# Folding softmax row sums on GpSimd instead of TensorE in a grouped-query attention block

## The chip, the cores and the metric

The kernel runs on one core of one Trainium2 chip. The metric is the device time of one execution in microseconds (us). Engines are called as in the profile: PE is TensorE, DVE is VectorE, ACT is ScalarE, POOL is GpSimd, SP is SyncE, which here issues almost all loads. PEld is TensorE's weight load, and a q behind an engine's name (SPq) marks its queue of instructions. Within 2% counts as the same.

## The reference

Two independent attention blocks, A and B, each on its own inputs, with the results side by side:

```python
q = (x @ wq)                      # x: 16 x 32 x 1024, wq: 1024 x 4096 -> 32 heads of 128
scores = q @ k^T * 128 ** -0.5    # 4 key/value heads, 512 cached keys, 8 query heads share each
p = softmax(scores)
out = (p @ v) @ wo                # wo: 4096 x 1024
```

All inputs are bfloat16. One *slot* of the kernel is one pair of batch and key/value head: 512 keys against 8 x 32 = 256 query columns. There are 64 slots for A and 64 for B.

## The kernel before

Scores are computed transposed, with keys on partitions, so the softmax sums run over partitions. There is no maximum: the exponent gets a constant shift, and a check at the end guards it. In each slot PE does four score matmuls and four value matmuls, and between them a stream of projection matmuls (`units`) is fed in, six or seven to a slot. The sums are formed in three steps: DVE reduces each 32 x 32 block of the exponentials (`partial_sums`), then the four key chunks of a pair of slots (`chunk_sums`), and PE adds the four partition quadrants with a matmul against stacked identities (`fold_sums`). That matmul also spreads the result to all quadrants. Of the tiles named below, kT holds the transposed keys and v_sb the values of a group of four slots, p_sb the exponentials of one slot; blk is the pool of the weights and of what the projections read and write.

```python
def load_k(j): ...   # one group j = 4 slots; kT tile from a pool of 3, DMA transposes on nc.sync
def load_v(j):
    v_sb = v_tiles[j] = kv.tile([P, GRP, KC, DH], BF16, name="v_sb")     # pool of 3
    nc.sync.dma_start(out=v_sb[:], in_=...)
# ... cut ...
def chunk_sums(j): ...            # DVE: parts -> cs
def fold_sums(j):
    sums = pair[j] = psum.tile([P, 2 * REP], FP32, name="sums", tag="sums", bufs=1)
    nc.tensor.matmul(sums[:], lhsT=fold[...], rhs=cs[...], start=True, stop=True)
def reciprocals(j): ...           # DVE: rall = 1 / sums, then transpose to r
def values(i): ...                # PE: 4 matmuls into ob, ONE PSUM bank for a pair of slots
def normalize(j): ...             # DVE: oT = r * ob, frees ob
# ... cut ...
for j in range(2, 2 * NG // GRP):
    at(GRP * (j - 1), load_k, j)          # at(slot, ...): place in program order
    at(GRP * (j - 1) + 2, load_v, j)
for c4 in range(3, 16): ...               # wq tiles of 1 MB, blk pool
for nh in range(NH):
    for hg in range(HKV):                 # wo tiles of 1 MB, blk pool
        at(NG - 12 + nh * 8 + hg * 2, load_wo, 0, nh, hg)
        at(NG + 20 + nh * 18 + hg, load_wo, 1, nh, hg)
# ... cut ...
for i in range(total_slots + 3):
    j, odd = divmod(i, 2)
    if live: do_loads(i); scores(i)
    run(units, 1)
    if not odd and 1 <= j <= NG: chunk_sums(j - 1)
    if i >= 3: values(i - 3)
    if odd and 1 <= j <= NG: reciprocals(j - 1)
    if not odd and j >= 2: normalize(j - 2)
    run(units, 5)
    if not odd and 1 <= j <= NG: fold_sums(j - 1)
    if live: partial_sums(i)
    run(units, 1 - (i % 4 == 3))
```

A load's place in this plan orders it in the SP queue. It is issued when SP has got that far and the buffer that it overwrites has been read for the last time.

## Time and profile before

Time before: 350.65 us, the median of three runs (350.25 to 350.69).

The page's first part gives the span and the busy time of each engine, with its share of the span and its number of instructions.

```profile
span 349.1 us, 5460 instructions
...
PE 340.7 (98%) x2163; PEld 221.0 (63%) x2204; DVE 283.4 (81%) x421; ACT 179.6 (51%) x196; POOL 8.9 (3%) x21
```

PE is busy all the time. Its lines in the timeline show start, length, engine, source line and operands; matmuls overlap, so the starts are what to subtract.

```profile
101.71 0.60 PE L371 MATMUL s_ps<-qT,kT 128*128 128x256 bf16 x4
...
102.80 1.24 PE L312 MATMUL q_ps<-xT,wq_sb 128*128 128x512 bf16 x5
103.69 0.36 PE L407 MATMUL sums<-cs,fold 128*128 128x16 f32 x1
103.91 0.39 PE L312 MATMUL q_ps<-xT,wq_sb 128*128 128x512 bf16 x1
104.14 0.60 PE L371 MATMUL s_ps<-qT,kT 128*128 128x256 bf16 x4
...
106.31 0.60 PE L371 MATMUL s_ps<-qT,kT 128*128 128x256 bf16 x4
```

A slot goes from one group of score matmuls (s_ps) to the next. (A few matmul records are missing from this trace, among them one projection matmul after 102.1; its weight load is listed at 102.04. So the first slot has seven.) The slot at 101.71 holds a fold (103.69) and lasts 2.43 us; the one at 104.14 has one projection matmul fewer and no fold and lasts 2.17 us. Over 28 periods of four slots (34.73 to 298.45 us) the mean is 9.42 us.

The groups of instructions give busy time and the mean of one in ns, then the idle time before them and what ended it.

```profile
L407 PE MATMUL sums<-cs,fold 128*128 128x16 f32 x64 | 22.9, 357 | 0.1
L399 DVE TENSOR_REDUCE cs<-parts 128x16 fp32r<-128x64 f32 x64 | 16.9, 264 | 2.2
L416 DVE RECIPROCAL rall<-sums 128x16 f32<-128x16 f32 x64 | 14.1, 220 | 0.0
L407 PEld LDWEIGHTS sums<-cs,fold 128*128 128x128 f32 x64 | 12.1, 190 | 8.3 <-DVE cs L399 0.9
```

The fold is 22.9 us of listed matmul time. Because matmuls overlap, that is not its price. The last number of the last line: twice PE's weight load waited for the chunk sums, 0.9 us in all.

### The profile page before, as it was taken

How to read it: one execution, taken by the hardware profiler on the slowest of the kernel's cores; microseconds unless marked ns; L12 is line 12 of the kernel's file. 1: busy time of each engine (PE TensorE's matmuls, PEld its weight loads, DVE VectorE, ACT ScalarE, POOL GpSimd, SP SyncE). 2: the span in 40 equal slices, each digit the busy share in tenths (PEclk: the TensorE clock that was granted, in tenths of full speed). 3: DMA queues.
4: the chain of work that ended last, by engine and by line, in shares of the span. 5: the costliest groups of instructions: out<-in, count | busy, mean ns of one | idle time of the engine just before them, and what ended most of it. 6: DMA issues, size and time to landing. Idle time of an engine off the chain costs nothing.

```text
span 349.1 us, 5460 instructions
## 1 busy us (share of the span) xinstructions
PE 340.7 (98%) x2163; PEld 221.0 (63%) x2204; DVE 283.4 (81%) x421; ACT 179.6 (51%) x196; POOL 8.9 (3%) x21
## 2 busy tenths in 40 slices
PE   8999999999999999999999999999999999999995
PEld 4556666666666666666666666666666666666554
DVE  2218888988988898898889999999989999899710
ACT  2247667666666666666654454454454445445000
POOL 0000000000000000000000000000000000000010
PEclk9999999999999999999999999999999999999999
DMA  7999999999996999999999659996579975400000
GB/s 242 275 251 339 181 274 264 254 269 249 270 214 176 199 233 233 296 275 210 305 313 192 175 126 289 348 199 122 135 258 287 284 182 97 116 17 0 15 32 20
DMA packets 125085, 71.70 MB, mean 205 GB/s; under 512 B 73632, under 2 KB 124064, under 8 KB 125056
## 3 DMA queue, kind: packets, MB, share of 16 engines
q1 hardware_dynamic: 122848, 68.24, 81.1%
q0 software_dynamic: 720, 1.97, 1.6%
q10 hardware_dynamic: 1488, 1.11, 1.1%
q8 instruction: 18, 0.29, 0.4%
q14 instruction: 11, 0.09, 0.1%
HBM read 51.38 MB, written 2.10 MB: 153 GB/s over the span
## 4 chain that ended last, share of the span: by engine, by line
PE 94%; DMA 3%; issue 1%; DVE 1%; ACT 0%; SPq 0%
PE f_ps L331 31%; PE q_ps L312 30%; PE ob L431 16%; PE s_ps L371 16%; DMA wq_sb<-in_A_wq_dram 2%; DMA x_sb<-in_A_x_dram 1%; DVE parts L390 0%; PE sums L407 0%; DVE o_sb L343 0%; ACT o_sb L341 0%; DVE cs L399 0%; PE ok_ps L614 0%; SPq L651 0%
## 5 line engine op out<-in xcount | busy, mean ns | idle before, releaser
L379 ACT ACTIVATE p_sb<-s_ps,shift 128x1024 bf16<-128x1024 f32 x128 | 142.5, 1114 | 113.1 <-PE s_ps L371 100.4
L390 DVE TRANSPOSE_TENSOR_REDUCE parts<-p_sb 128x32 f32<-128x1024 bf16 x128 | 158.2, 1236 | 21.5 <-ACT p_sb L379 20.9
L331 PE MATMUL f_ps<-wo_sb,oT 128*128 128x512 bf16 (+1 forms) x524 | 127.9, 367 | 0.4
L312 PE MATMUL q_ps<-xT,wq_sb 128*128 128x512 bf16 x475 | 124.8, 380 | 0.6
L371 PE MATMUL s_ps<-qT,kT 128*128 128x256 bf16 x512 | 76.8, 273 | 0.9
L431 PE MATMUL ob<-p_sb,v_sb 128*128 128x256 bf16 x512 | 76.8, 273 | 0.6
L331 PEld LDWEIGHTS <-oT 128*128 128x128 bf16 x544 | 53.0, 98 | 33.8
L312 PEld LDWEIGHTS <-wq_sb 128*128 128x128 bf16 x496 | 48.3, 98 | 35.1 <-DMA wq_sb<-in_A_wq_dram 0.6
L371 PEld LDWEIGHTS <-kT 128*128 128x128 bf16 x512 | 56.9, 113 | 20.9
L431 PEld LDWEIGHTS <-v_sb 128*128 128x128 bf16 x512 | 50.1, 98 | 19.8 <-DVE oT L453 0.3
L453 DVE TENSOR_TENSOR oT<-r,ob 128x512 bf16<-128x512 f32 x64 | 43.9, 685 | 12.7 <-PE ob L431 9.3
L320 ACT CAST qT<-q_ps 128x512 bf16<-128x512 f32 x62 | 36.1, 583 | 23.7 <-PE q_ps L312 20.8
L418 DVE STREAM_TRANSPOSE r<-rall 128x512 f32<-128x512 f32 x64 | 45.5, 711 | 2.2
L407 PE MATMUL sums<-cs,fold 128*128 128x16 f32 x64 | 22.9, 357 | 0.1
L343 DVE CAST o_sb<-f_ps 128x512 bf16<-128x512 f32 (+1 forms) x16 | 10.8, 673 | 10.8 <-PE f_ps L331 10.0
L399 DVE TENSOR_REDUCE cs<-parts 128x16 fp32r<-128x64 f32 x64 | 16.9, 264 | 2.2
L407 PEld LDWEIGHTS sums<-cs,fold 128*128 128x128 f32 x64 | 12.1, 190 | 8.3 <-DVE cs L399 0.9
L345 POOL DMA_DIRECT2D out_dram<-o_sb x15 | 8.2, 549 | 329.7 <-DVE o_sb L343 299.0
L416 DVE RECIPROCAL rall<-sums 128x16 f32<-128x16 f32 x64 | 14.1, 220 | 0.0
L341 ACT CAST o_sb<-f_ps 128x256 bf16<-128x256 f32 x1 | 0.4, 372 | 22.1 <-PE f_ps L331 22.1
L497 DVE COPY xT<-xT_ps 128x512 bf16<-128x512 bf16 x4 | 1.7, 424 | 5.3 <-PE xT_ps L493 5.3
L484 PE MATMUL warm_ps<-warm 128*128 128x512 bf16 x10 | 4.2, 580 | 1.3 <-DVE warm L230 1.3
(26 smaller groups left out, 22.8 us busy)
## 6 DMA issues: line engine op xcount, KB each, us to landing
v_sb<-in_A_v_cache_dram SPq DMA_DIRECT2D x16, 512.0 KB, 4.9
wq_sb<-in_B_wq_dram SPq DMA_DIRECT2D x8, 1024.0 KB, 6.5
wo_sb<-in_A_wo_dram SPq DMA_DIRECT2D x8, 1024.0 KB, 7.6
v_sb<-in_B_v_cache_dram SPq DMA_DIRECT2D x16, 512.0 KB, 4.2
wo_sb<-in_B_wo_dram SPq DMA_DIRECT2D x8, 1024.0 KB, 9.2
wq_sb<-in_A_wq_dram SPq DMA_DIRECT2D x7, 1024.0 KB, 8.0
out_dram<-o_sb POOLq DMA_DIRECT2D x15, 128.0 KB, 3.1
kT<-in_A_k_cache_dram SPq DMA_TRANSPOSE x64, 4.5
```

What stands on the lines that cost most here:

```text
L312: nc.tensor.matmul(ps[:], lhsT=w[:, dc, (h % 4) * DH:(h % 4 + 1) * DH], rhs=xT[pr][:, dc, :], start=(dc == 0), stop=(dc == DC - 1),)
L320: nc.scalar.copy(out=qT[pr, g][:, :, hl, :], in_=ps[:].rearrange("p (b s) -> p b s", s=SQ),)
L331: nc.tensor.matmul(ps[:, 0:width], lhsT=oT[pr, tt][:, h, :], rhs=wo_tiles[pr, nh, h // REP][:, h % REP, off:off + width], start=(h == 0), ...
L371: nc.tensor.matmul(s_ps[:, c, :], lhsT=kT[:, i % GRP, c, :], rhs=qT[pr, g][:, b, :, :].rearrange("p h s -> p (h s)"), start=True, stop=True,)
L379: nc.scalar.activation(out=p_sb[:], in_=s_ps[:], func=ACTF.Exp, bias=shift[:], scale=SCALE)
L390: nc.vector.tensor_reduce(out=parts[j][:, q, :, :].rearrange("p c h -> p (c h)"), in_=st[i]["p"][:].rearrange("p c (h s) -> p (c h) s", s=SQ),
L399: nc.vector.tensor_reduce(out=cs[:], in_=parts.pop(j)[:].rearrange("p q c h -> p q h c"), axis=AX.X, op=ALU.add,)
L407: nc.tensor.matmul(sums[:], lhsT=fold[:].rearrange("p r s -> p (r s)"), rhs=cs[:].rearrange("p q h -> p (q h)"), start=True, stop=True,)
L416: nc.vector.reciprocal(out=rall[:, j, :], in_=pair.pop(j)[:])
L418: nc.vector.transpose(out=r[:].rearrange("p n s -> p (n s)"), in_=rall[:, j, :].unsqueeze(2).to_broadcast([P, 2 * REP, SQ]),)
L431: nc.tensor.matmul(ob[j][:, q, :], lhsT=v_sb[:, i % GRP, c, :], rhs=st[i]["p"][:, c, :], start=(c == 0), stop=(c == KC - 1),)
L453: nc.vector.tensor_tensor(out=out, in0=rcp.pop(j)[:].rearrange("p (q h) s -> p q h s", h=REP), in1=ob.pop(j)[:].rearrange("p q (h s) -> p ...
```

## The change

The intent is to take the fold off the busiest engine and put it on an idle one. POOL adds the chunks, copies the quadrants beside each other, adds them, and copies the result back to all four quadrants, once for four slots. The longer path needs more lag, so values run six slots behind instead of three. That takes eight p_sb buffers instead of five. The diff makes three more edits around it: blk 20 to 19 tiles, v_sb three to two buffers, and new places for the loads.

```diff
-            blk = enter(tc.tile_pool(name="blk", bufs=20))
+            blk = enter(tc.tile_pool(name="blk", bufs=19))
...
-                v_sb = v_tiles[j] = kv.tile([P, GRP, KC, DH], BF16, name="v_sb")
+                v_sb = v_tiles[j] = kv.tile([P, GRP, KC, DH], BF16, name="v_sb", bufs=2)
...
-                p_sb = work.tile([P, KC, QW], BF16, name="p_sb", bufs=5)
+                p_sb = work.tile([P, KC, QW], BF16, name="p_sb", bufs=8)
...
-            def chunk_sums(j): ...                       (cut)
             def fold_sums(j):
-                nc.tensor.matmul(sums[:], lhsT=fold..., rhs=cs..., start=True, stop=True)
+                nc.gpsimd.tensor_tensor(out=a[:], in0=p[:, 0:2], in1=p[:, 2:4], op=ALU.add)
+                nc.gpsimd.tensor_tensor(out=cs[:], in0=a[:, 0], in1=a[:, 1], op=ALU.add)
+                for r in range(NQ):
+                    nc.gpsimd.tensor_copy(out=g[:, r], in_=cs[quadrant(r)])
+                nc.gpsimd.tensor_tensor(out=g2[:], in0=g[:, 0:2], in1=g[:, 2:4], op=ALU.add)
+                nc.gpsimd.tensor_tensor(out=g3[:], in0=g2[:, 0], in1=g2[:, 1], op=ALU.add)
+                for r in range(NQ):
+                    nc.gpsimd.tensor_copy(out=sums[quadrant(r)], in_=g3[...])
...
-                at(GRP * (j - 1), load_k, j)
-                at(GRP * (j - 1) + 2, load_v, j)
+                at(GRP * (j - 2) + 2, load_k, j)
+                at(GRP * j + 1, load_v, j)
...
-            for i in range(total_slots + 3):
+            for i in range(total_slots + 6):
...
-                if not odd and 1 <= j <= NG: chunk_sums(j - 1)
-                if i >= 3: values(i - 3)
-                if odd and 1 <= j <= NG: reciprocals(j - 1)
-                if not odd and j >= 2: normalize(j - 2)
+                if q == 0 and 1 <= j <= total_slots // 4: fold_sums(j - 1)
+                if i >= 6: values(i - 6)
+                if q == 2 and 1 <= j <= total_slots // 4: reciprocals(j - 1); spread(2 * j - 2)
+                if q == 0 and j >= 2: spread(2 * j - 3)
+                if q % 2 == 1 and i >= 7: normalize((i - 7) // 2)
```

(The lines of the loop are joined here to save room.)

More of the change, by code (lines that the diff above doesn't have):

```diff
@@ L232, in fast_path @@
             make_identity(nc, ident[:])
-            fold = const.tile([P, P // QD, QD], FP32R, name="fold")
-            for r in range(P // QD):
-                rs = slice(r * QD, (r + 1) * QD)
-                nc.vector.tensor_copy(
-                    out=fold[rs],
-                    in_=ident[rs, rs].unsqueeze(1).to_broadcast([QD, P // QD, QD]),
-                )
             one_col = const.tile([P, 1], FP32, name="one_col")
@@ L382, in scores @@
                 st[i] = {"p": p_sb}
-            parts, rcp, pair = {}, {}, {}
+            parts, rcp, quad = {}, {}, {}
             def partial_sums(i):
-                j, q = divmod(i, 2)
+                j, q = divmod(i, 4)
                 if q == 0:
-                    parts[j] = work.tile([P, 2, KC, REP], FP32, name="parts")
+                    parts[j] = work.tile([P, 4, KC, REP], FP32, name="parts")
                 nc.vector.tensor_reduce(
@@ L394, in partial_sums @@
                 )
-            def chunk_sums(j):
-                cs = pair[j] = work.tile([P, 2, REP], FP32R, name="cs")
-                with nc.allow_low_precision(reason="float32r holds the float32 sum"):
-                    nc.vector.tensor_reduce(
-                        out=cs[:], in_=parts.pop(j)[:].rearrange("p q c h -> p q h c"),
-                        axis=AX.X, op=ALU.add,
-                    )
-            def fold_sums(j):
-                cs = pair[j]
-                sums = pair[j] = psum.tile([P, 2 * REP], FP32, name="sums", tag="sums", bufs=1)
-                nc.tensor.matmul(
-                    sums[:],
-                    lhsT=fold[:].rearrange("p r s -> p (r s)"),
-                    rhs=cs[:].rearrange("p q h -> p (q h)"),
-                    start=True,
-                    stop=True,
-                )
@@ L415, in reciprocals, with quadrant, fold_sums @@
-            def reciprocals(j):
-                nc.vector.reciprocal(out=rall[:, j, :], in_=pair.pop(j)[:])
+            NQ = P // QD
+            def quadrant(r):
+                return slice(r * QD, (r + 1) * QD)
+            def fold_sums(j):
+                p = parts.pop(j)[:].rearrange("p q c h -> p c q h")
+                a = work.tile([P, 2, 4, REP], FP32, name="a", bufs=1)
+                nc.gpsimd.tensor_tensor(out=a[:], in0=p[:, 0:2], in1=p[:, 2:4], op=ALU.add)
+                cs = work.tile([P, 4, REP], FP32, name="cs", bufs=1)
+                nc.gpsimd.tensor_tensor(out=cs[:], in0=a[:, 0], in1=a[:, 1], op=ALU.add)
+                g = work.tile([QD, NQ, 4, REP], FP32, name="g", bufs=1)
+                for r in range(NQ):
+                    nc.gpsimd.tensor_copy(out=g[:, r], in_=cs[quadrant(r)])
+                g2 = work.tile([QD, 2, 4, REP], FP32, name="g2", bufs=1)
+                nc.gpsimd.tensor_tensor(out=g2[:], in0=g[:, 0:2], in1=g[:, 2:4], op=ALU.add)
+                g3 = work.tile([QD, 4, REP], FP32, name="g3", bufs=1)
+                nc.gpsimd.tensor_tensor(out=g3[:], in0=g2[:, 0], in1=g2[:, 1], op=ALU.add)
+                sums = quad[j] = work.tile([P, 4 * REP], FP32, name="sums", bufs=1)
+                for r in range(NQ):
+                    nc.gpsimd.tensor_copy(
+                        out=sums[quadrant(r)], in_=g3[:].rearrange("p q h -> p (q h)")
+                    )
@@ L417, in reciprocals, with spread @@
+            def reciprocals(j):
+                nc.vector.reciprocal(
+                    out=rall[:, 2 * j:2 * j + 2, :].rearrange("p j n -> p (j n)"),
+                    in_=quad.pop(j)[:],
+                )
+            def spread(j):
                 r = rcp[j] = work.tile([P, 2 * REP, SQ], FP32, name="r")
@@ L578, in fast_path @@
             total_slots = 2 * NG
-            for i in range(total_slots + 3):
+            for i in range(total_slots + 6):
                 live = i < total_slots
-                j, odd = divmod(i, 2)
+                j, q = divmod(i, 4)
                 if live:
@@ L585, in fast_path @@
                 run(units, 1)
-                if not odd and 1 <= j <= NG:
-                    chunk_sums(j - 1)
-                if i >= 3:
-                    values(i - 3)
-                if odd and 1 <= j <= NG:
-                    reciprocals(j - 1)
-                if not odd and j >= 2:
-                    normalize(j - 2)
+                if q == 0 and 1 <= j <= total_slots // 4:
+                    fold_sums(j - 1)
+                if i >= 6:
+                    values(i - 6)
+                if q == 2 and 1 <= j <= total_slots // 4:
+                    reciprocals(j - 1)
+                    spread(2 * j - 2)
+                if q == 0 and j >= 2:
+                    spread(2 * j - 3)
+                if q % 2 == 1 and i >= 7:
+                    normalize((i - 7) // 2)
                 run(units, 5)
-                if not odd and 1 <= j <= NG:
-                    fold_sums(j - 1)
                 if live:
```

## The prediction

> **What bounds it now.** The PE stream. The page gives PE 340.7 us of 349.1 (98%), the chain of waits is 94% PE, PEclk is full throughout, and the waits list shows almost nothing that PE waits for. In the timeline the work repeats every four slots (32 attention matmuls, 27 projection matmuls, 2 folds): 34.73 to 298.45 us in 28 periods, 9.42 us each. Between 100 and 110 us a slot with six projection matmuls and no fold takes 2.17 us, with seven and no fold 2.39, with seven and a fold 2.43. DVE is 81% busy (8.7 us per period), ACT 51%, POOL 3%.
>
> **What the change takes off PE.** The 64 fold matmuls. The groups list 22.9 us of matmul and 12.1 us of weight load, but those overlap their neighbours. By the slot lengths a fold delays the stream by 0.04 to 0.05 us (2.43 against 2.39; or 9.42 minus 27 x 0.216 and 32 x 0.109, halved). 64 x 0.045 = 2.9 us: the gain, 0.8%. No other PE work changes; values six slots behind only moves work into the tail.
>
> **DVE.** Chunk sums (64 x 0.264 = 16.9 us) go, 64 reciprocals (14.1 us) become 32 of about 0.24. Busy falls from 283 to about 260 us. Off the path: worth nothing itself.
>
> **POOL.** Gains 32 x 12 instructions, of which the trace shows none; its memsets and affine select took 0.10 to 0.29 us. With the two-input rate of the Trainium skill, GPSIMD Engine Reference, section 3.1 (about 2.6 cycles per element, 1.2 GHz) on a 0.1 us base, the four adds take 0.16 to 0.25 us, the eight copies about 0.15; with waits between dependent steps I estimate 2.5 to 4 us per chain, 80 to 130 us busy. The chain starts when the fourth partial sum is done (about 0.8 us into slot 4j); the reciprocal is wanted two slots later: 4.7 us. If it is late, DVE stalls in order, but normalize waits for PE anyway and the single ob bank must be free only at the next pair of values: about 1.5 us more. So the chain is hidden below about 6 us; above that PE stalls every four slots. The same page (Specifications) says GpSimd shares SBUF interfaces with VectorE when DVE uses two ports or two SBUF inputs; normalize reads one operand from PSUM, so I expect DVE instructions at most 3% longer. No run here shows it yet.
>
> **Loads.** v_sb goes from three to two buffers: a load can go once the values two groups back end in slot 4j+1, and is needed in 4j+6: 11.5 us, against a landing of 3.7 to 9.5 us. kT comes two slots earlier. The blk pool at 19 exceeds the 18 tiles that I count live at once. Few or no DMA waits on PE.
>
> **Predicted time:** 348.0 us, eight in ten between 346.8 and 351.0. Chances: faster by over 2%: 0.03; within 2%: 0.87; slower: 0.10.
>
> **What would show each step.** A PE period of 9.32 to 9.34 us, fold lines gone; DVE busy near 260 us, partial sums still 1.24 us; POOL 25 to 40% busy, its chain from first add to last copy under 4.7 us; reciprocal hardly waiting for POOL; no PE wait for v_sb or oT; the tail unchanged.
>
> **What would make it wrong.** POOL instructions of 0.5 us or more with long hand-overs: the chain exceeds 6 us, DVE waits for sums, normalize is late, PE waits for ob; 1 us over the limit could cost 32 us. DVE slowed by POOL. v loads late behind transposes in the in-order SP queue: 1 to 3 us. POOL's output DMA issues, waiting for o_sb in order, delaying a chain in the second half.

## More of the kernel before

The SP queue's timeline in the stretch in which the output weights (wo_sb, 1 MB each) are loaded:

```profile
152.75 9.52 SPq L288 DMA_TRANSPOSE kT<-in_B_k_cache_dram  x1
162.31 0.58 SPq L267 DMA_DIRECT2D wo_sb<-in_A_wo_dram  x1
162.99 0.53 SPq L294 DMA_DIRECT2D v_sb<-in_B_v_cache_dram  x1
163.61 0.45 SPq L267 DMA_DIRECT2D wo_sb<-in_A_wo_dram  x1
164.16 8.96 SPq L288 DMA_TRANSPOSE kT<-in_B_k_cache_dram  x1
```

Here the length is the time for which the instruction held the SP queue. One kT transpose held it for 9 us. The v_sb load at 162.99 is that of group 16, whose first use by PE is at 179.8 us.

## The result

The changed kernel took 350.93 us (median of four runs, 350.44 to 351.89) against 350.54 us for the kernel before on the same chip. The ratio is 1.0016 with a 95% interval of 0.9991 to 1.0040, so the two are the same. In this document a ratio is the mean time of one kernel's fast runs over the mean of the other's of the same rounds, so it is not quite the ratio of the medians quoted. The time lies inside the predicted range, at its edge, but the forecast gain of 2.7 us is not there.

The changed kernel's page, same lines as before:

```profile
span 348.7 us, 5721 instructions
...
PE 340.5 (98%) x2140; PEld 214.9 (62%) x2140; DVE 261.7 (75%) x321; ACT 180.0 (52%) x196; POOL 96.9 (28%) x405
```

The span is 0.4 us shorter. DVE fell to 261.7 us and POOL is at 28%, both as forecast. PE in its timeline:

```profile
102.06 0.60 PE L364 MATMUL s_ps<-qT,kT 128*128 128x256 bf16 x4
...
104.22 0.60 PE L364 MATMUL s_ps<-qT,kT 128*128 128x256 bf16 x4
...
106.61 0.60 PE L364 MATMUL s_ps<-qT,kT 128*128 128x256 bf16 x4
...
108.99 0.60 PE L364 MATMUL s_ps<-qT,kT 128*128 128x256 bf16 x4
...
111.38 0.60 PE L364 MATMUL s_ps<-qT,kT 128*128 128x256 bf16 x4
```

From 102.06 to 111.38 there are four slots in 9.32 us, as forecast, and no fold. One POOL chain, and the DVE instructions around its reader:

Columns as before; in brackets stand the idle time before and what ended it.

```profile
105.33 0.32 POOL L397 TENSOR_TENSOR a<-parts 128x64 f32<-128x64 f32 x1 [5.96 <-DVE parts L383]
105.73 0.25 POOL L399 TENSOR_TENSOR cs<-a 128x32 f32<-128x32 f32 x1
106.05 0.93 POOL L402 COPY g<-cs 32x32 f32<-32x32 f32 x4
107.06 0.31 POOL L404 TENSOR_TENSOR g<-g 32x64 f32<-32x64 f32 x1
107.44 0.24 POOL L406 TENSOR_TENSOR g<-g 32x32 f32<-32x32 f32 x1
107.75 0.94 POOL L409 COPY sums<-g 32x32 f32<-32x32 f32 x4
```

```profile
108.50 1.24 DVE L383 TRANSPOSE_TENSOR_REDUCE parts<-p_sb 128x32 f32<-128x1024 bf16 x1
109.66 0.31 DVE L414 RECIPROCAL rall<-sums 128x32 f32<-128x32 f32 x1
```

The chain lasts from 105.33 to 108.69, 3.36 us, and the reciprocal asks for the sums at 109.66, when they have been there for about 1 us. So the fold on POOL is hidden: over the whole run the reciprocal waited for it once, 1.6 us. The time went elsewhere. The list of waits (who waited, for whom, total us, times, longest) has lines that the kernel before did not have:

```profile
PEld L434 <- DMA v_sb<-in_B_v_cache_dram: 2.0, 1, 2.0
...
PE ob L434 <- DMA v_sb<-in_B_v_cache_dram: 1.6, 1, 1.6
...
PEld L364 <- DMA kT<-in_B_k_cache_dram: 1.5, 1, 1.5
...
PE s_ps L364 <- DMA kT<-in_B_k_cache_dram: 1.0, 1, 1.0
```

Each wait appears twice, once for the weight load and once for the matmul. PE's own timeline shows the first:

```profile
181.61 0.38 PE L324 MATMUL f_ps<-wo_sb,oT 128*128 128x512 bf16 x1
181.83 0.60 PE L434 MATMUL ob<-p_sb,v_sb 128*128 128x256 bf16 x4
...
184.00 0.38 PE L324 MATMUL f_ps<-wo_sb,oT 128*128 128x512 bf16 x1
185.96 0.61 PE L434 MATMUL ob<-p_sb,v_sb 128*128 128x256 bf16 x4 [1.59 <-DMA v_sb<-in_B_v_cache_dram]
```

At 181.61 the values follow the projection matmul by 0.22 us; at 184.00 they should do so at about 184.21 and come at 185.96, which is 1.75 us late. The second wait is at 283.08 us, where the scores come at 284.22, 1.14 us late. Together 2.9 us, as much as the folds had been reckoned to cost, and most of the 3.1 us by which this span is longer than that of e1 below (345.6 us), which has no such waits. The chain of waits (start, length, what) leads from the late values back through the load to the SP queue:

```profile
165.52 0.23 PE q_ps L305
165.75 1.05 SPq L287
...
166.85 7.10 SPq L281
...
174.00 0.57 SPq L260
...
174.62 0.58 SPq L260
...
175.30 10.62 DMA v_sb<-in_B_v_cache_dram
...
185.96 0.61 PE ob L434 x4
```

The buffer that this load overwrites was last read by the value matmuls that run in slot 65 (those of slot 59, six behind), which ended at 173.1 us. SP was then still issuing the kT transpose (until 173.95) and two weight loads, so the v_sb load was issued at 175.30, 2.2 us after its buffer was free, and took 10.6 us to land. PE wanted it at 184.21, 11.1 us after the buffer came free.

The following table is worked out from the traces: for the load of a group, the time between its landing and the first weight load of that group on PE (the slack, us). Zero means that PE waited.

| kernel | v_sb of group 12 | 14 | 15 | 16 | 17 | 26 | kT of group 28 |
|---|---|---|---|---|---|---|---|
| before | 14.8 | 14.4 | 12.7 | 9.5 | 7.4 | 16.2 | 6.9 |
| changed | 7.1 | 1.6 | 0.5 | 0.0 | 1.0 | 2.2 | 0.0 |

The slack fell by 6 to 14 us, for the six v_sb loads shown by 10.4 us on average: about one group of four slots (9.3 us). It is used up only where the 1 MB weight loads are bunched.

### The profile page after: what moved, and what is told of

Its sections match the earlier page's. It is cut to its first block, busy times and chain, and to the rows that moved or that the text cites. A ratio compares the mean times of both kernels' runs of the same rounds, so it can differ in the third digit from the quotient of the medians.

```text
span 348.7 us, 5721 instructions
## 1 busy us (share of the span) xinstructions
PE 340.5 (98%) x2140; PEld 214.9 (62%) x2140; DVE 261.7 (75%) x321; ACT 180.0 (52%) x196; POOL 96.9 (28%) x405
## 4 chain that ended last, share of the span: by engine, by line
PE 88%; DMA 7%; SPq 3%; issue 0%; DVE 0%; ACT 0%; DVEq 0%
PE q_ps L305 29%; PE f_ps L324 27%; PE s_ps L364 14%; PE ob L434 14%; DMA kT<-in_B_k_cache_dram 4%; DMA v_sb<-in_B_v_cache_dram 3%; SPq L281 2%; PE q_ps L510 1%; PE warm_ps L487 1%; SPq L260 1%; PE xT_ps L496 1%; SPq L287 1%; DVE xT L500 0%; ACT o_sb L334 0%; DVE warm L230 0%
## 5 line engine op out<-in xcount | busy, mean ns | idle before, releaser
L383 DVE TRANSPOSE_TENSOR_REDUCE parts<-p_sb 128x32 f32<-128x1024 bf16 x128 | 158.4, 1238 | 23.4 <-ACT p_sb L372 22.0
L324 PE MATMUL f_ps<-wo_sb,oT 128*128 128x512 bf16 (+1 forms) x544 | 132.1, 367 | 0.0
L305 PE MATMUL q_ps<-xT,wq_sb 128*128 128x512 bf16 x496 | 127.8, 379 | 0.0
L456 DVE TENSOR_TENSOR oT<-r,ob 128x512 bf16<-128x512 f32 x64 | 43.8, 685 | 34.1 <-PE ob L434 33.9
L397 POOL TENSOR_TENSOR a<-parts 128x64 f32<-128x64 f32 x32 | 10.1, 316 | 172.8 <-DVE parts L383 172.8
L421 DVE STREAM_TRANSPOSE r<-rall 128x512 f32<-128x512 f32 x64 | 44.2, 691 | 1.1
L409 POOL COPY sums<-g 32x32 f32<-32x32 f32 x128 | 26.1, 204 | 6.0
L402 POOL COPY g<-cs 32x32 f32<-32x32 f32 x128 | 25.9, 202 | 6.0
L414 DVE RECIPROCAL rall<-sums 128x32 f32<-128x32 f32 x32 | 10.0, 313 | 1.7 <-POOL sums L409 1.6
L404 POOL TENSOR_TENSOR g<-g 32x64 f32<-32x64 f32 x32 | 9.9, 310 | 2.6
L399 POOL TENSOR_TENSOR cs<-a 128x32 f32<-128x32 f32 x32 | 8.1, 252 | 2.5
```

The source lines that it names most:

```text
L305: nc.tensor.matmul(ps[:], lhsT=w[:, dc, (h % 4) * DH:(h % 4 + 1) * DH], rhs=xT[pr][:, dc, :], start=(dc == 0), stop=(dc == DC - 1),)
L324: nc.tensor.matmul(ps[:, 0:width], lhsT=oT[pr, tt][:, h, :], rhs=wo_tiles[pr, nh, h // REP][:, h % REP, off:off + width], start=(h == 0), ...
L383: nc.vector.tensor_reduce(out=parts[j][:, q, :, :].rearrange("p c h -> p (c h)"), in_=st[i]["p"][:].rearrange("p c (h s) -> p (c h) s", s=SQ),
L402: nc.gpsimd.tensor_copy(out=g[:, r], in_=cs[quadrant(r)])
L409: nc.gpsimd.tensor_copy(out=sums[quadrant(r)], in_=g3[:].rearrange("p q h -> p (q h)"))
L421: nc.vector.transpose(out=r[:].rearrange("p n s -> p (n s)"), in_=rall[:, j, :].unsqueeze(2).to_broadcast([P, 2 * REP, SQ]),)
```

## The experiments

Theory A: two v_sb buffers instead of three cost one group of prefetch and hold back the in-order SP queue, and the gain is spent on waits for late loads. Rival B: the new places of the loads in program order do it. Rival C: the POOL work slows loads or DVE. Unless a result says otherwise, each experiment was timed in five rounds and compared with the kernel before on the same chip. Results were correct except where said.

### e1_three_v

```diff
-    v_sb = v_tiles[j] = kv.tile([...], BF16, name="v_sb", bufs=2)
+    v_sb = v_tiles[j] = kv.tile([...], BF16, name="v_sb")        # the changed kernel, otherwise untouched
```

> The changed kernel with three v_sb buffers again, nothing else different. In the changed kernel's trace PE loses 1.75 us at 184 us to a v_sb load and 1.14 us at 283 us to a kT load, together 2.9 us, as much as the 64 fold matmuls saved. Theory A (two v_sb buffers hold back the in-order SP queue, so that the loads behind a v_sb load go later): both waits vanish, 347.6 to 348.3 us, PE period still 9.32 us. Theory B (the new places of the loads in program order are to blame, not the number of buffers): one or both waits stay, 349.5 to 351. Theory C (the POOL work delays loads or DVE): no change, about 350.9.

347.50 us against 351.04, ratio 0.9898 (0.9884 to 0.9912). No PE wait for v_sb or kT is left, and the chain of waits is PE from end to end:

```profile
PE 98%; ACT 0%; DVE 0%; issue 0%; DVEq 0%
```

The kernel still fits in SBUF with the third buffer. Slack at group 16 is 5.8 us for v_sb; the smallest anywhere is 4.9. Theory A stands; B falls, as the places of the loads are those of the change.

### e2_loads_only

The kernel before with everything of the change except the POOL fold: blk 19, v_sb 2, p_sb 8, lag 6, loads at the new places; chunk sums and the fold matmul stay.

```diff
-    blk bufs=20, p_sb bufs=5, v_sb of 3;  load_k at GRP*(j-1), load_v at GRP*(j-1)+2     (summarised)
+    blk bufs=19, p_sb bufs=8, v_sb of 2;  load_k at GRP*(j-2)+2, load_v at GRP*j+1
-                if i >= 3: values(i - 3)
-                if not odd and j >= 2: normalize(j - 2)
+                if i >= 6: values(i - 6)
+                if not odd and j >= 3: spread(j - 3)          # the transpose, taken out of reciprocals
+                if odd and i >= 7: normalize((i - 7) // 2)
```

> The kernel before with everything of the change except the fold: folding by matmul stays on PE, POOL idle; values six slots behind, two v_sb buffers, 19 blk tiles, loads at the new places. Theories A and B: the fold's 2.9 us are not saved and the DMA waits of about 2 to 3 us come in, 352.5 to 354 us, with PE waits for v_sb or kT in the trace. Theory C: no such waits without POOL work, 350.3 to 351.

351.47 against 351.04, ratio 1.0011 (0.9998 to 1.0024). This missed what A expected: 2 to 3 us of waits were forecast and 0.4 us came. Its list of waits has 0.9 us for kT (weight loads and matmuls counted both), 1.3 us for wq_sb loads of A, and none for v_sb; the slack at group 16 is 0.7 us. So the same loads are just in time while PE still does the folds.

### e3_no_pool

The changed kernel with the POOL chain replaced by a constant tile of sums; the result is wrong.

```diff
-                ... the twelve POOL instructions of fold_sums ...
+                parts.pop(j)
+                quad[j] = sums_const          # memset once to 2.0 ** 60
```

> The changed kernel without the POOL chain: the reciprocal reads a constant tile, so the result is wrong on purpose; all loads and buffers as in the changed kernel. Theories A and B: time stays at 350 to 351.5 us, with PE waits for v_sb and kT of 2 to 3 us still there. Theory C: 347.5 to 348.5, waits gone.

350.50 us, ratio 0.9997 (0.9962 to 1.0031), from five fast runs that scatter widely (349.3 to 353.5; a sixth was slow). The waits are all there (v_sb 4.0 us and kT 2.9 us in the list, weight loads and matmuls counted both), without any POOL arithmetic. Rival C falls.

### e4_before_two_v

```diff
-    v_sb = v_tiles[j] = kv.tile([...], BF16, name="v_sb")
+    v_sb = v_tiles[j] = kv.tile([...], BF16, name="v_sb", bufs=2)   # the kernel before, otherwise untouched
```

> The kernel before with two v_sb buffers instead of three, nothing else. Theory A: the queue is held back by the values two groups back, PE waits for v_sb or kT appear, 352 to 355 us. Theory B: the old places of the loads protect it, within 0.5 us of before. Theory C: within 0.5 us of before.

357.24 against 351.04, ratio 1.0189 (1.0171 to 1.0207): somewhat more than A expected. PE waits for kT five times, up to 3.2 us each, never for v_sb. In the old plan kT of the next group stands behind v_sb in the queue, and a v_sb load that waits for its buffer keeps it there. So the old places of the loads are no protection. In e2, with two buffers, the new places and the longer lag together, the cost was 0.4 us; which of the two saves the rest was not tested apart.

### e5_v_on_act_queue

```diff
-    at(GRP * j + 1, load_v, j)                 # issued by nc.sync
+    at(GRP * j + 2, load_v, j, nc.scalar)      # two v_sb buffers, issued by ACT
```

> The changed kernel, two v_sb buffers, with the v_sb loads issued from the ACT queue one slot later instead of from SP. Theory A1 (the one in-order SP queue does the harm: v_sb waits there behind a kT issue of 7 to 9 us, and what follows waits behind v_sb): both PE waits vanish, 347.3 to 348.3 us, smallest slack of a load over 2 us. Theory A2 (it is the depth of prefetch itself: with two buffers a load cannot be asked for more than about 11.5 us before its use, whatever the queue, and landings grow to 10 us while weights are loaded): waits for v_sb stay, 349.5 to 351.

348.92 against 350.72, ratio 0.9965 (0.9932 to 0.9998; six runs, one of them 352.2). Both halves of theory A are real. The waits for kT are gone (smallest slack 2.6 us), so holding the SP queue was what hurt kT. The v_sb loads still come late twice (1.9 us of weight-load waits), with landings of up to 12.2 us. The load of group 26 was issued 0.04 us after its buffer came free (266.52 us) and still landed too late: the landing alone used up the window. The Trainium skill, in Trainium Kernel Development and Optimization, section Key Constraints, says that DMAs issued from several engines "all run on the same 16 DMA engines and interleave", and that issuing from several saves only the sequencer's issue time. This run agrees: another queue removed the waiting in line and left the landing time.

### e6_weights_spread

```diff
-    at(NG - 12 + nh * 8 + hg * 2, load_wo, 0, nh, hg)
-    at(NG + 20 + nh * 18 + hg, load_wo, 1, nh, hg)
+    at(NG - 12 + hg * 2 + nh * (16 + hg), load_wo, 0, nh, hg)
+    at(NG + 20 + nh * 18 + hg * 3, load_wo, 1, nh, hg)
```

> The changed kernel, two v_sb buffers, all loads on SP, but the wo_sb loads of 1 MB no longer bunched: the second four of A at slots 68 to 77 instead of 60 to 66, those of B three slots apart instead of one. If the waits come only where the thin prefetch meets a burst of weights (in the changed kernel v_sb loads land with 0 to 2 us to spare at 165 to 195 us and around 242 and 279 us, and with 6 to 7 us elsewhere): both waits vanish, 347.3 to 348.3 us. If two buffers are too few by themselves: waits elsewhere, 349.5 or more.

347.35 against 350.72, ratio 0.9907 (0.9892 to 0.9921), with two v_sb buffers and no DMA wait for v_sb or kT. The slack at group 16 is 6.9 us. So two buffers are enough if the weights are not bunched. The waits come where a thin prefetch meets a burst of 1 MB loads.

### e7_after_again

The changed kernel once more, beside the others on this chip; no edit.

> The changed kernel itself on this chip, beside the others. Expected 350.5 to 351.5 us with PE waits of 2 to 3 us for v_sb and kT in its trace, as in its first profile. If its waits differ by over 1 us here, single profiles must not be compared closer than that.

349.63 against 350.72, ratio 0.9967 (0.9955 to 0.9980). The trace has the same two waits (slack 0 at v_sb of group 16 and kT of group 28). So between the two sets of runs the changed kernel is 0.2% slower to 0.3% faster than before, and its median is 2.3 us above that of e6 in the same rounds.

### e8_fold_three_v

```diff
-    v_sb = v_tiles[j] = kv.tile([...], BF16, name="v_sb", bufs=2)   # in e2
+    v_sb = v_tiles[j] = kv.tile([...], BF16, name="v_sb")
```

> The fold still by matmul on PE, values six slots behind and loads at the new places, but three v_sb buffers: against the run with three v_sb buffers and the fold on POOL (347.5) it prices the fold alone, on loads that are never late. If a fold costs the stream 0.045 us: 2.9 us more, 350.2 to 350.7 us, PE period 9.41 us. If the fold had cost more through its wait for the chunk sums: over 351.

351.06 against 350.72, ratio 1.0012 (0.9999 to 1.0025). Against e6 of the same rounds, where the loads are in time too, the fold costs 1.05% of 350.7 us, 3.7 us or 0.058 us for each. The expectation was 2.9 us, or more if the fold's wait for the chunk sums counts. The traces tell the two apart. From the scores of slot 1 to those of slot 127, with 63 folds between them, PE takes 294.71 us in e8 and 291.53 us in e6. Of these 3.2 us, 0.44 us are two slots in which the chunk sums came late (2.76 and 2.54 us instead of 2.43); the rest is 0.043 us a fold. So the matmul's own price is what was predicted. What it leaves out are waits of PE's weight load for the chunk sums: four in this trace, 1.7 us in all on that engine, of which only a part delays the stream. The two-by-two of fold and buffers (ratio to before):

| | three v_sb | two v_sb, weights bunched |
|---|---|---|
| fold on PE | 1.0012 (e8) | 1.0011 (e2) |
| fold on POOL | 0.9898 (e1) | 1.0016 and 0.9967 (the change, twice) |

The costs do not add. The third buffer is worth nothing with the fold on PE, and 0.7 to 1.2% without it. Taking the fold off is worth 1.1% with it, and little or nothing without.

### e9_three_v_spread

The edits of e1 and e6 together:

```diff
-    v_sb = v_tiles[j] = kv.tile([...], BF16, name="v_sb", bufs=2)   # in e6
+    v_sb = v_tiles[j] = kv.tile([...], BF16, name="v_sb")
```

> Three v_sb buffers and the wo_sb loads spread, both. If the stream is all that is left, nothing more is to be had than from either alone: 347.2 to 347.7 us. If loads still cost something in some executions: up to 0.5 us less and a narrower range.

347.64 against 350.44, ratio 0.9922 (0.9909 to 0.9935). Nothing more is to be had: either remedy alone already leaves only the PE stream.

### e10_chain_plus_two and e11_chain_plus_four

```diff
-                for r in range(NQ):                # last four copies of the chain, on e1
+                for r in list(range(NQ)) * 3:      # e10;  * 5 in e11
```

> Three v_sb buffers, and the last four copies of each POOL chain done three times: the chain grows from 3.36 to about 5.25 us. In the changed kernel it ends about 1 us before DVE asks for the sums. The prediction's account (hidden below about 6 us): time unchanged, 347.3 to 348 us; the reciprocal waits about 1 us for POOL in each of 32 chains, PE waits for nothing new. If instead POOL work itself slows DVE or the loads, or the limit is at 4.7 us: 350 or more.

> The same with those copies done five times: chain about 7.15 us, still under the 9.32 us period. The prediction's account (1 us over a limit of about 6 us costs up to 32 us): about 1 us per period, 370 to 385 us, with PE waiting for oT. If the lag of six slots gives more room than reckoned: 348 to 355.

e10: 362.36 against 350.44, ratio 1.0338 (1.0323 to 1.0353; three rounds). e11: 429.89, ratio 1.2259 (1.2239 to 1.2278). Both are far over what was expected. In e10, the waits, DVE, and POOL from the start of one chain to that of the next:

```profile
DVE rall L414 <- POOL sums L409: 61.0, 32, 4.1
...
PE ob L434 <- DVE oT L456: 11.0, 28, 1.6
```

```profile
114.45 0.35 DVE L414 RECIPROCAL rall<-sums 128x32 f32<-128x32 f32 x1 [1.92 <-POOL sums L409]
114.84 0.71 DVE L421 STREAM_TRANSPOSE r<-rall 128x512 f32<-128x512 f32 x1
115.48 1.20 DVE L383 TRANSPOSE_TENSOR_REDUCE parts<-p_sb 128x32 f32<-128x1024 bf16 x1
116.60 0.65 DVE L456 TENSOR_TENSOR oT<-r,ob 128x512 bf16<-128x512 f32 x1
```

```profile
118.55 0.32 POOL L397 TENSOR_TENSOR a<-parts 128x64 f32<-128x64 f32 x1 [4.13 <-DVE parts L383]
...
120.97 3.08 POOL L409 COPY sums<-g 32x32 f32<-32x32 f32 x12
128.19 0.32 POOL L397 TENSOR_TENSOR a<-parts 128x64 f32<-128x64 f32 x1 [4.13 <-DVE parts L383]
```

The reciprocal waits 1.92 us for POOL, and normalize (L456) comes only after the transpose and a whole partial sum behind it, at 116.60, so PE's next values wait 0.37 us. The chain of 5.5 us (118.55 to 124.05) gives a period of 9.64 us (118.55 to 128.19), 0.32 over 9.32; over the whole run it is 0.46 (362.36 less 347.50, by 32). From the end of one chain to the start of the next POOL is idle for 4.13 us here, and in e11, with a chain of 7.55 us, again for 4.13 us in most periods. In that time DVE runs, one after the other, the reciprocal, a transpose, a partial sum, normalize and the partial sum that completes the next four, so chain and DVE form a loop. So the room for the chain is 9.32 less 4.13, or 5.2 us, not 6 (4.6 us in the periods in which DVE also copies an output tile and the idle time is 4.74 us). From e10 to e11 the chain grows by 2.05 us and the time by 67.5 us over 32 periods, 2.1 us each: beyond the limit each microsecond is paid in full. (In e11's profile the granted PE clock was 0.94, so its slope is less exact.)

### e12_idle_fold, e13_idle_fold_early, e14_idle_fold_late, e15_late_start

These ask why the loads were in time in e2 and not in the changed kernel. e12 puts a fold matmul of constant data back in each second slot of the changed kernel, unused. e13 does so only before slot 48, e14 only from slot 48 on. e15 has no folds and starts the first slot 1.5 us later, by seven warm-up matmuls.

```diff
+                if q % 2 == 0 and 2 <= i <= total_slots:     # e13: 2 <= i < 48;  e14: 48 <= i <= total_slots
+                    idle_fold()
+            warm_up(7)                                           # e15 alone, and no idle_fold
```

> The changed kernel with 64 fold matmuls of constant data back in their places on PE, the result unused: the stream is slowed as before, the sums still come from POOL, two v_sb buffers. If the pace of PE decides how much the thin prefetch costs (with the fold on PE, its loads-only run lost 0.4 us, the changed kernel 2 to 3): PE waits for DMA shrink to under 1 us and the time is 350.5 to 351.7 us, hardly above the changed kernel. If the two costs add: 353 to 354.5.

> The changed kernel with idle fold matmuls only in slots 2 to 46, before the stretch with the weights: PE comes to it about 1.1 to 1.3 us later and then runs at the fast pace. From the v_sb load of group 12 to the landing of that of group 16 the changed kernel takes 49.8 to 50.3 us, with folds on PE 47.9. If the loads end at a fixed time whatever PE does (theory D1: DMA has work carried over from earlier): that stretch shrinks to about 49, the v_sb wait at group 16 to about 0.5 us, time about 350.3. If the pace inside the stretch decides (D2): 50 us and the wait of 1.75 us stay, 351.5 to 352.

> The same with idle fold matmuls only from slot 48 on. D1: the stretch stays at 49.5 to 50 us, the v_sb wait stays over 1 us, 351 to 352. D2: the stretch falls to 48 us, no v_sb wait, 349.5 to 350.5.

> The changed kernel with seven more warm-up matmuls (1.5 us) before the first slot, no folds. D1: PE later by 1.5 us finds the loads there, waits fall by about 1.5 us at group 16, time within 0.6 us of the changed kernel. D2: waits unchanged, 1.5 us longer.

| run | us | ratio to before | 95% interval | v_sb of group 12 issued to group 16 landed |
|---|---|---|---|---|
| changed, e7, e3 | | | | 50.1, 49.8, 50.3 |
| e2 | 351.47 | 1.0011 | 0.9998 to 1.0024 | 47.9 |
| e12 | 350.31 | 0.9991 | 0.9980 to 1.0003 | 48.0 |
| e13 | 350.60 | 1.0001 | 0.9983 to 1.0019 | 49.4 |
| e14 | 352.55 | 1.0040 | 1.0022 to 1.0059 | 51.9 |
| e15 | 353.25 | 1.0063 | 1.0048 to 1.0078 | 50.3 |

e12 shows again that the costs do not add: with 64 extra matmuls on PE its ratio lies between the two of the changed kernel (0.9967 and 1.0016), because the waits for v_sb are gone (slack 0.6 us at group 16) and that for kT is 0.4 us. But neither explanation of that held. If the loads ended at a fixed time (D1), a late start would have been free; e15 is 0.5 to 1.0% above the changed kernel, at least the 1.5 us by which it was late, with both waits still there. If the pace inside the stretch decided (D2), e14 would have had the short stretch; it had the longest, with a v_sb wait of about 3 us. (The profiled run of e14 was its slowest, 355.3 us; but its median of 352.55 us lies above D2's 349.5 to 350.5 as well.) e13 lies between the two. What sets whether this stretch of loads takes 48 or 50 us stays open. Longer slots explain only that PE wants group 16 about 0.5 us later in e2 than in the changed kernel (48.6 us after the issue for group 12, against 48.1), not that the loads end 2 us sooner.

## Why the prediction was wrong

The fold's price on PE: right. The period fell from 9.42 to 9.32 us. The estimate of 2.9 us was low by 0.8 us (e8: 3.7). A fold's own 0.045 us was right (0.043); left out were its waits for the chunk sums, of which the trace of before already listed 0.9 us. With loads in time the changed fold gives 347.5 us, against a prediction of 348.0.

DVE off the path, busy near 260 us: right (261.7). Partial sums 1238 ns against 1236, normalize 685 against 685, so POOL work did not lengthen DVE. The partial sums that ran for over 60% of their time beside POOL's instructions took 1241 ns, those that ran beside none 1236. The Trainium skill, GPSIMD Engine Reference, section Specifications, limits the contention with VectorE to its two-port modes and to two SBUF inputs; this trace agrees in that normalize, with one input in PSUM, took 684 ns beside POOL work and without it. No run here shows the contention itself.

The POOL chain: right in length (3.36 us in an estimate of 2.5 to 4) and hidden. Its limit was mis-sized: "hidden below about 6 us" measured about 5.2 (e10, e11). The account left out the partial sum that stands between the reciprocal and normalize on DVE, and that the next chain cannot start before both are done (the 4.13 us of e10).

The loads: here the prediction failed. The step reads "a load can go once the values two groups back end in slot 4j+1, and is needed in 4j+6: 11.5 us, against a landing of 3.7 to 9.5 us ... Few or no DMA waits on PE." The window was right (11.1 us at group 16). Wrong was to set it against the landing times of the old trace. First, a load whose buffer is free is not yet issued: it stood 2.2 us in the SP queue behind a kT transpose and two weight loads. Secondly, it landed after 10.6 us, in the stretch with the wo_sb loads. 2.2 + 10.6 against 11.1 is the wait of 1.7 us. The second wait has the same cause at one remove: v_sb loads that wait for PE hold the queue, and the kT load of group 28 went out at 270.7 us, where the run with three buffers issued it at 261.6; landings of 13.5 and 11.8 us then ended late and in time. e1 and e6 show the cause by removing it in two ways; e1 also rules out rival B, for it keeps the new places, and e3 rules out rival C. The prediction named this risk with the right size ("v loads late behind transposes in the in-order SP queue: 1 to 3 us") and then gave it no place in the sum. That the measured time still lies in the range, 0.07 us from its end, is owed to the range's width and not to the sum.

The changed fold with three v_sb buffers, or with the weights spread, beats both kernels by about 1% (0.9898 and 0.9907).

## What to carry to other kernels

When a change pays for itself with a buffer, work out the slack of every load that uses that buffer, group by group, and look for the groups where it meets another burst; a mean or a median landing says nothing about them. In an in-order queue the time to compare is from the last read of the buffer to the landing, including what stands ahead in the queue, and a load that waits for its buffer delays everything behind it. For work moved to an idle engine, find its deadline by following the reader's engine to the next thing that PE waits for, with everything that stands in between; past the deadline here each microsecond was paid in full.

## What the Trainium skill lacked or had wrong

- GPSIMD Engine Reference, section 3.1, gives two-input adds at 2048 elements only. For small ones the runs show 252 ns at 32 elements and 316 ns at 64: a base of about 0.19 us, larger than the 0.1 us taken here from memsets, and 2.0 ns an element, about 2.4 cycles at the stated 1.2 GHz, which agrees with the page's 2.6. A 32 x 32 copy between quadrants takes 0.20 us, with 0.24 us from start to start in the changed kernel and 0.26 us in e10; no page that I read has that.
- DMA: Bandwidth & Descriptors has sequencer times of a DMA transpose only in its part on another chip, for small tiles and from SBUF to SBUF; how long a large one from HBM holds the queue that issues it here, it does not say. In the changed kernel one kT transpose of a whole group of B held SP for 3.3 to 9.6 us, and a v_sb load of 0.5 MB landed after 3.8 to 10.6 us; with the weights spread (e6) the longest was 8.9 us.
- TensorE: Matmul & The Clock Gate has no figure that I found for a float32r matmul of 16 columns in a stream of bfloat16 ones. It is listed at 357 ns here and delayed the stream by 0.04 to 0.05 us.
